# One load of x instead of two, and a shorter last load of w_down, in an attention and GLU decode kernel

## The chip, the cores and the metric

The kernel runs on one core of a Trainium2 chip. The metric is the device time of one execution in microseconds (us). All numbers of the profile come from one further execution, taken with the hardware profiler.

## The reference

Everything is float32. One token with D = 512 numbers goes through a layer norm; the result feeds an attention over a cache of 8192 keys and values for each of 32 heads of 128 numbers, and a gated linear unit (GLU) with F = 1376 hidden numbers.

```
xn = (x - mean(x)) / sqrt(var(x) + 1e-5)                 # x: 512 numbers
q  = (xn @ wq)            -> 32 heads x 128              # wq: 512 x 4096
p  = softmax(q . k_cache / sqrt(128))  over 8192 keys    # k_cache: 32 x 8192 x 128
s  = concat_heads(p @ v_cache) @ wo                      # v_cache: 32 x 8192 x 128, wo: 4096 x 512
h  = sigmoid(xn @ w_gate) * (xn @ w_up)                  # w_gate, w_up: 512 x 1376
g  = silu(h @ w_down)                                    # w_down: 1376 x 512
out = x + s * g
```

## The kernel before

**Data.** The caches are 128 MiB each, the weights some 24 MiB together. Each number is read once and used once, so nearly all that the kernel does is move them from HBM to SBUF and multiply once.

**Memory.** Three slots of 64 KB a partition (`slots[0..2]`, 8 MiB each) hold what is streamed. A load of keys takes two heads (a *pair*, 16 pairs in all, `NP`): heads 2i and 2i+1 lie on partitions 0 to 63 and 64 to 127, each partition with 128 consecutive keys. Keys of pair i go to slot i % 2, the values of each pair but the last to slot 2, in which `wq` lay at first. The values of the last pair go to slot 0, and then `w_gate`, `w_up` and the first 1280 rows of `w_down` to slot 2, and `wo`, in six pieces, to slot 1.

**Queues.** All those loads are issued by SyncE (SP), in the order of the program, each behind a wait for its slot: `load_keys(i)` waits until the scores of pair i-2 have been summed, `load_values(i-1)` until TensorE has used the values of pair i-2. `load(eng, name, dst, src, *after)` (L131 is its `dma_start`) gives each load a semaphore. ScalarE (ACT) issues the small ones: the two loads of x at the start, and `place(i)`, which spreads the two heads of a finished pair over eight partitions of `o_all`.

**The start.** x is needed in two forms. `x_col` is x as columns: 128 partitions with 4 numbers each, `x_col[p, k] = x[4p + k]`; the layer norm works on it and makes `xn`, which TensorE takes as weights. `x_row` has x as rows: partitions 0, 32, 64 and 96 hold 128 numbers each, and every other partition zero; only the last addition (L418) reads it. The layer norm is a chain that goes to and fro: VectorE sums (L180), TensorE adds over the partitions by a matmul with ones (L182), VectorE subtracts the mean and squares (L184 to L190), TensorE adds again (L192), ScalarE takes the root (L194), VectorE scales (L196, L198). Then 64 matmuls with `wq` make the queries (L206), ScalarE copies them (L211), TensorE spreads each row over the partitions (L218), and ScalarE copies that to `qb` (L225), two pairs at a time; `copies[0]` is what pairs 0 and 1 wait for.

**The pairs.** For each pair VectorE multiplies the keys in place with the queries (L281) and sums over the 128 numbers of each key (L282). TensorE, VectorE and ScalarE find the maximum and the powers (L284, L246, L276, L248, L294, L296), TensorE takes the values (64 matmuls, L255), and VectorE scales the two heads (L288, L289).

**The tail.** After the last pair TensorE makes gate and up (L356), 32 numbers of the hidden row at a time on each of four partition groups; the first 1280 columns make groups of 320, and the last 96 are in columns 320 to 351 of groups 1 to 3. For that VectorE sets group 0 of those columns to zero (L348), and TensorE waits for it. After the sigmoid and the product, eleven 32x32-block transposes (L366, L367) turn the hidden row into columns, `hid`. The down product is made of ten matmuls with 128 rows of `w_down` (`wd_t`) and one with `wd_last`. `wd_last` holds the last 128 rows of `w_down`, of which the first 32 have been taken already; `hid` is zero there.

```python
    ld_d = load(SP, "wd", wd_last, w_down[F - P:, :])           # P = 128
    ...
        ins = PE.matmul(big[0][g:g + 1, :], hid[:, c, 0:1], wd_t[:, c, :] if c < FP else wd_last, ...)
```

The sums of four partition groups are folded (L371, L377), the gate is made (L390, L392), and the product with `wo` follows, each piece as it lands (L402, then L406). L416 multiplies by the gate, L418 adds `x_row`, and SP stores the result (L422).

Of the kernel before, what the change touches and what calls it, by code (L numbers as in the profile page):

```python
# [13 lines left out]
P = 128  # L14
# [4 lines left out]
def kernel(  # L19
# [15 lines left out]
    F = w_gate.shape[1]  # L35
    KT = D // P
# [3 lines left out]
    NG = 4  # L40
    GP = P // NG
# [3 lines left out]
    NQ = H * Dh // QT  # L45
# [6 lines left out]
    FP = F // P  # L52
    FL = F - FP * P
    FW = FP * GP
    FH = FW + GP
# [4 lines left out]
    PE, DVE, ACT, SP, POOL = nc.tensor, nc.vector, nc.scalar, nc.sync, nc.gpsimd  # L60
# [8 lines left out]
    def sb(name, *shape):  # L69
        return nc.alloc_sbuf_tensor(name, [P, *shape], F32)[:]  # L70

    def bank(name, rows, cols):
        return nc.alloc_psum_tensor(name, [rows, cols], F32)[:]


    x_col, xc, sq, xn = (sb(n, KT) for n in ("x_col", "xc", "sq", "xn"))
    st, eps_t = sb("st", 8), sb("eps_t", 1)
    mx, nb, rs, rl = sb("mx", 4), sb("nb", 2), sb("rs", 1), sb("rl", 1)

# [2 lines left out]
    x_row, g_row = sb("x_row", GC), sb("g_row", GC)  # L82
    ones, ident = sb("ones", P), sb("ident", P)
# [5 lines left out]
    wd_last = q_all[:, :D]  # L89
# [7 lines left out]
    hid = o1[:, :(FP + 1) * GP].rearrange("p (c i) -> p c i", i=GP)  # L97
# [3 lines left out]
    big = [bank(f"big{i}", P, QT) for i in range(2)]  # L101
# [7 lines left out]
    def semaphore(name):  # L109
        sems.append(nc.alloc_semaphore(name))  # L110
        return sems[-1]
# [11 lines left out]
    pe, dve, act, pool = (Steps(n) for n in ("s_pe", "s_dve", "s_act", "s_pool"))  # L123
    loads = {}

    def load(eng, name, dst, src, *after):
        wait(eng, *after)
        if name not in loads:
            loads[name] = [semaphore(f"s_{name}"), 0]
        loads[name][1] += 16  # L130
        eng.dma_start(dst, src).then_inc(loads[name][0], 16)  # L131
        return loads[name][0], loads[name][1]

    def wait(eng, *steps):
        for s in steps:
            if s is not None:
                eng.wait_ge(*s)
# [7 lines left out]
    xv = x.rearrange("a b d -> (a b d)")  # L145
# [9 lines left out]
    def load_keys(i, *after):  # L155
        ld_k[i] = load(SP, f"k{i % 2}", slots[i % 2], rows_of(k_cache, i), *after)
# [5 lines left out]

    load_keys(0)
    load_keys(1)
    ld_x = load(ACT, "x", x_col, xv.rearrange("(p k) -> p k", k=KT))


    c_ones = dve(DVE.memset(ones, 1.0))
    c_xrow = dve(DVE.memset(x_row, 0.0))
    ld_xr = load(ACT, "xr", x_row[0:P:GP, :], xv.rearrange("(g c) -> g c", g=NG), c_xrow)  # L170
    c_eps = dve(DVE.memset(eps_t, EPS))
    c_id = pool(POOL.memset(ident, 0.0))
    wait(POOL, c_id)
# [2 lines left out]
    c_big = [dve(DVE.memset(t, 0.0)) for t in big]  # L176


    wait(DVE, ld_x)
    t = dve(DVE.reduce_sum(st[:, 0:1], x_col, axis=AX.X))  # L180
    wait(PE, t)
    t = pe(PE.matmul(pt[:, 0:1], ones, st[:, 0:1], start=True, stop=True))  # L182
# [19 lines left out]
    for k in range(KT):  # L202
        for b in range(NQ // NG):
            for g in range(NG):
                c = (b * NG + g) * QT
                ins = PE.matmul(big[b][g * GP:g * GP + 1, :], xn[:, k:k + 1], wq_t[:, k, c:c + QT],  # L206
                                start=(k == 0), stop=(k == KT - 1))
# [6 lines left out]
    spreads, copies = {}, {}  # L214
    for t in range(NQ):
        b, g = divmod(t, NG)
# [117 lines left out]
    wd_t = t[:, 2 * KT * F:2 * KT * F + FP * D].rearrange("p (c e) -> p c e", e=D)  # L334
    ld_g = load(SP, "wg", wg_t, w_gate.rearrange("(p k) f -> p k f", k=KT), (valued, NP - 1))
    ld_u = load(SP, "wu", wu_t, w_up.rearrange("(p k) f -> p k f", k=KT))
    load(SP, "wd", wd_t, w_down[:FP * P, :].rearrange("(p r) e -> p r e", r=FP))
    ld_d = load(SP, "wd", wd_last, w_down[F - P:, :])
    wo_t = slots[(NP - 1) % 2].rearrange("p (r e) -> p r e", e=D)
    ld_o = []  # L340
    for n, (r0, r1) in enumerate(zip((0,) + W_ENDS, W_ENDS)):
# [1 line left out]
                         summed[NP - 1] if n == 0 else None))  # L343


    g0 = (P - FL) // GP
    wait(DVE, copies[NQ - 1])
    c_zero = dve(DVE.memset(big[1][:g0 * GP, FW:FH], 0.0))  # L348
    wait(PE, c_zero)
    rows = []  # L350
    for dst, src, ld in ((big[0], wg_t, ld_g), (big[1], wu_t, ld_u)):
        wait(PE, ld)
        for c0, f0, w, g1 in ((0, 0, FW, 0), (FW, F - P, GP, g0)):
            for k in range(KT):
                for g in range(g1, NG):
                    ins = PE.matmul(dst[g * GP:g * GP + 1, c0:c0 + w], xn[:, k:k + 1],  # L356
                                    src[:, k, f0 + g * w:f0 + (g + 1) * w], start=(k == 0), stop=(k == KT - 1))
        rows.append(pe(ins))
# [22 lines left out]
    wait(PE, t, ld_d)  # L381
    for c in range(FP + 1):
        g = c % NG * GP
        ins = PE.matmul(big[0][g:g + 1, :], hid[:, c, 0:1], wd_t[:, c, :] if c < FP else wd_last,
                        start=(c < NG), stop=(c + NG > FP))
    t = to_fold(pe(ins))
    wait(DVE, t)
# [4 lines left out]
    c_gate = dve(DVE.tensor_mul(g_row, g_row, big[1][:, :GC]))  # L392
# [4 lines left out]
    for ld, r1 in zip(ld_o, W_ENDS):  # L397
        wait(PE, ld)
        for r in range(r0, r1):
            if r < W_FOLD:  # L400
                g = r % NG * GP
                ins = PE.matmul(big[0][g:g + 1, :], o_all[:, r:r + 1], wo_t[:, r, :],  # L402
                                start=(r < NG), stop=(r + NG >= W_FOLD))
                continue
            for g in range(NG):
                ins = PE.matmul(acc[g * GP:g * GP + 1, :], o_all[:, r:r + 1], wo_t[:, r, g * GC:(g + 1) * GC],  # L406
                                start=(r == W_FOLD), stop=(r == WR - 1))
# [4 lines left out]
        if r1 == W_FOLD:  # L412
            parts = to_fold(pe(ins))
        r0 = r1
    wait(DVE, pe(ins), c_gate, ld_xr)
    t = dve(DVE.tensor_mul(g_row, g_row, acc))  # L416
    wait(DVE, t)
    t = dve(DVE.tensor_add(g_row, g_row, x_row))  # L418
# [39 lines left out]
```

## Time and profile before

| what | before |
|---|---|
| time, median of 3 runs | 687.56 us (687.45 to 687.59) |
| profiled execution: span from the first to the last instruction | 685.6 us |
| what the median has over that span | 1.96 us |
| VectorE busy | 574.0 us (84%) |
| TensorE busy | 222.1 us (32%) |
| mean busy share of the 16 DMA engines by the packets of queue q1 (SP) | 99.1% |
| packets of queue q10 (ACT) | 408, with 0.02 MB |
| bytes read from HBM | 293.74 MB, 428 GB/s over the span |

The page gives no time of its own for the profiled execution, only its span. The median of the runs is 1.96 us more than that span: what lies before the first and after the last instruction. A change that shortens the span by so much is taken to shorten the time by the same.

In a timeline row the columns are: start and duration in us, engine (PEld is the weight load of TensorE; SPq and ACTq are the DMA issues of SyncE and ScalarE), line, operation, what is written from what, and in brackets the idle time before it with what ended it. In a row of DMA issues the last number is the time from issue to landing.

### The profile page before, as it was taken

Reading aid. Unit: us, or ns where it says so; the run is one execution under the profiler, and the core shown is the slowest. Engines: PE = TensorE matmul, PEld = TensorE weight load, DVE = VectorE, ACT = ScalarE, POOL = GpSimd, SP = SyncE. Lnnn points to the kernel's source line nnn. Section 1 sums busy time; section 2 is a strip of 40 time slices with the busy share of each in tenths; the row PEclk is TensorE's granted clock in tenths of the full one; section 3 lists DMA queues with packets and bytes.
Section 4 is the critical chain, followed back from the end, with each engine's and each line's share of the span. In section 5 each row is a group of like instructions: output and inputs, shape, how many; then the busy total and the mean of one; then the engine's idle time right before and its main releaser. Section 6 shows DMA issues by size and latency. Waiting matters only on the chain.

```text
span 685.6 us, 3694 instructions
## 1 busy us (share of the span) xinstructions
PE 222.1 (32%) x1570; PEld 62.7 (9%) x1570; DVE 574.0 (84%) x136; ACT 40.9 (6%) x122; POOL 0.7 (0%) x6
## 2 busy tenths in 40 slices
PE   0550230605041140505042140506042140605656
PEld 0110000101010010101001010101000010101121
DVE  0159999999999999989898989989898989989220
ACT  0040100000000000000001010000001010000010
POOL 0000000000000000000000000000000000000000
PEclk9965575757566575757557575756657575756798
DMA  9999999999999999999999999999999999999996
GB/s 375 440 445 451 428 428 428 432 428 428 428 436 444 448 440 428 428 428 436 428 428 428 440 444 451 428 432 428 432 432 428 428 440 436 451 436 428 405 434 285
DMA packets 6614, 293.84 MB, mean 429 GB/s; under 512 B 1096, under 2 KB 1104, under 8 KB 1616
## 3 DMA queue, kind: packets, MB, share of 16 engines
q1 hardware_dynamic: 6200, 293.74, 99.1%
q10 hardware_dynamic: 408, 0.02, 0.0%
q8 instruction: 4, 0.07, 0.0%
q14 instruction: 2, 0.02, 0.0%
HBM read 293.74 MB, written 0.00 MB: 428 GB/s over the span
## 4 chain that ended last, share of the span: by engine, by line
DMA 37%; DVE 30%; PE 0%; SPq 0%; issue 0%
DMA slot<-in_A_k_cache_dram 31%; DVE slot L281 15%; DVE sc L282 15%; DMA slot<-in_A_wo_dram 6%; PE acc L406 0%; SPq L131 0%; PE pt L246 0%; PE acc L377 0%; DVE g_row L416 0%; DVE g_row L418 0%; DVE mx L276 0%
## 5 line engine op out<-in xcount | busy, mean ns | idle before, releaser
L281 DVE TENSOR_TENSOR slot<-slot,q_all 128x16384 f32<-128x16384 f32 x16 | 275.5, 17217 | 38.8 <-DMA slot<-in_A_k_cache_dram 38.8
L282 DVE TENSOR_REDUCE sc<-slot 128x128 f32<-128x16384 f32 x16 | 275.5, 17220 | 0.6
L255 PE MATMUL po<-slot,weights 128*8 128x512 f32 x1024 | 146.7, 737 | 232.1 <-PEq L242 231.5
L255 PEld LDWEIGHTS po<-slot,weights 128*8 128x8 f32 x1024 | 30.3, 103 | 335.3 <-issue 334.6
L246 PE MATMUL pt<-ident,mx 128*1 128x128 f32 x32 | 8.8, 374 | 148.6 <-PEq L242 148.6
L301 ACT COPY o<-po 128x512 f32<-128x512 f32 x16 | 9.4, 586 | 385.2 <-PE po L255 385.2
L260 PE MATMUL pn<-o,pick 128*2 128x128 f32 x128 | 16.5, 272 | 12.8 <-PEq L242 12.8
L180 DVE TENSOR_REDUCE st<-x_col 128x1 f32<-128x4 f32 x1 | 0.2, 157 | 20.7 <-DMA x_col<-in_A_x_dram 20.7
L246 PEld LDWEIGHTS pt<-ident,mx 128*1 128x1 f32 x32 | 1.8, 80 | 154.1 <-issue 154.1
L288 DVE RECIPROCAL rl<-pn 2x1 f32<-2x1 f32 x16 | 2.3, 146 | 14.6 <-PE pn L260 14.6
L294 ACT ACTIVATE nb<-pm 128x2 f32<-128x2 f32 x16 | 2.8, 173 | 190.4 <-PE pm L248 190.4
L416 DVE TENSOR_TENSOR g_row<-g_row,acc 128x128 f32<-128x128 f32 x1 | 0.3, 289 | 15.3 <-PE acc L406 15.3
L296 ACT ACTIVATE weights<-sc,nb 64x128 f32<-64x128 f32 x32 | 12.8, 399 | 0.9
L260 PEld LDWEIGHTS pn<-o,pick 128*2 128x2 f32 x128 | 9.9, 84 | 29.6 <-issue 27.2
L248 PE MATMUL pm<-mx,ones 1*128 1x2 f32 x32 | 8.8, 344 | 7.4 <-PEq L242 7.4
L402 PE MATMUL big<-slot,o_all 128*1 128x512 f32 x56 | 9.4, 765 | 4.8 <-DMA slot<-in_A_wo_dram 4.8
L250 PE MATMUL pn<-rs,half 128*2 128x1 f32 x32 | 3.0, 163 | 23.5 <-PEq L242 23.5
L218 PE MATMUL big<-q_all,ones 1*128 1x512 f32 x16 | 8.8, 850 | 1.6 <-ACT q_all L225 0.8
L206 PE MATMUL big<-slot,xn 128*1 128x512 f32 x64 | 9.0, 726 | 0.8 <-DVE xn L198 0.8
L248 PEld LDWEIGHTS pm<-mx,ones 1*128 1x128 f32 x32 | 7.9, 306 | 14.4 <-issue 14.4
L276 DVE TENSOR_REDUCE mx<-pt 1x2 f32<-1x128 f32 x16 | 4.5, 278 | 5.2 <-PE pt L246 5.0
L182 PE MATMUL pt<-st,ones 128*128 128x1 f32 x2 | 0.6, 362 | 23.4 <-DVE st L180 23.4
(61 smaller groups left out, 62.1 us busy)
## 6 DMA issues: line engine op xcount, KB each, us to landing
slot<-in_A_wo_dram SPq DMA_DIRECT2D x1, 3584.0 KB, 32.5
slot<-in_B_w_gate_dram SPq DMA_DIRECT2D x1, 2752.0 KB, 16.8
slot<-in_B_w_up_dram SPq DMA_DIRECT2D x1, 2752.0 KB, 22.8
slot<-in_B_w_down_dram SPq DMA_DIRECT2D x1, 2560.0 KB, 27.3
slot<-in_A_wo_dram SPq DMA_DIRECT2D x1, 2560.0 KB, 38.2
slot<-in_A_wo_dram SPq DMA_DIRECT2D x1, 1024.0 KB, 40.2
o_all<-on ACTq DMA_DIRECT2D x32, 0.5 KB
slot<-in_A_wo_dram SPq DMA_DIRECT2D x1, 512.0 KB, 40.9
```

The costliest lines, as they stand in the source:

```text
L206: ins = PE.matmul(big[b][g * GP:g * GP + 1, :], xn[:, k:k + 1], wq_t[:, k, c:c + QT], start=(k == 0), stop=(k == KT - 1))
L218: spreads[t] = pe(PE.matmul(big[t % 2], ones[g * GP:g * GP + 1, :], q_row[g * GP:g * GP + 1, b, :], start=True, stop=True))
L246: PE.matmul(pt[0:1, :], mx[:, 0:1], ident, start=True, stop=True).then_inc(turned, 1)
L248: PE.matmul(pm, ones[:1, :], mx[:1, 1:3], start=True, stop=True).then_inc(spread_m, 1)
L255: ins = PE.matmul(po[g * GP:g * GP + 2 * HT, :], weights[:, j // HT, :], v[:, j * Dh:(j + HT) * Dh], start=(j < HT * NG), stop=(j >= NB - ...
L260: ins = PE.matmul(pn[:, :Dh], pick[:, b:2 * HT:HT], o1[:, b * Dh:(b + 1) * Dh], start=(b == 0), stop=(b == HT - 1))
L276: DVE.reduce_max(mx[:1, 1:3], pt[0:1, :].rearrange("o (e p) -> o e p", e=2), axis=AX.X).then_inc(reduced, 1)
L281: wait(DVE, dve(DVE.tensor_mul(k, k, qb[:, i:i + 1, :].to_broadcast([P, NB, Dh]))))
L282: summed[i] = dve(DVE.reduce_sum(sc[i % 2], k, axis=AX.X))
L296: ACT.activation(weights[h, :, e * HT:(e + 1) * HT], sc[i % 2][h].rearrange("p (g b) -> p g b", b=HT), AF.Exp, bias=nb[h, e:e + 1], scale= ...
L301: ACT.copy(o1, po).then_inc(copied, 1)
L402: ins = PE.matmul(big[0][g:g + 1, :], o_all[:, r:r + 1], wo_t[:, r, :], start=(r < NG), stop=(r + NG >= W_FOLD))
```

## The change

**x.** The tile `x_col` and its load are gone. VectorE clears `x_row` first, then ScalarE issues the load of x as rows; `ones` is set after that instead of before. VectorE waits for that load, and turns the rows into columns with one transpose in blocks of 32x32: number 4i + k of row g goes to partition 32g + i, column block k. The result is put in `g_row`, which is not used otherwise before the tail; `x_col` is now a view of it with one number in every 32. The wait for the load ahead of the last addition is gone.

**The last rows of w_down.** 96 rows are loaded to 96 partitions instead of 128 to 128, and the last matmul of the down product takes 96 rows. The last 96 columns of gate and up are now in groups 0 to 2 instead of 1 to 3; as many matmuls as before. L348, which set a part of a bank to zero, and the two waits around it are gone.

```diff
-    x_col, xc, sq, xn = (sb(n, KT) for n in ("x_col", "xc", "sq", "xn"))
+    xc, sq, xn = (sb(n, KT) for n in ("xc", "sq", "xn"))
...
-    ld_x = load(ACT, "x", x_col, xv.rearrange("(p k) -> p k", k=KT))
-    c_ones = dve(DVE.memset(ones, 1.0))
     c_xrow = dve(DVE.memset(x_row, 0.0))
     ld_xr = load(ACT, "xr", x_row[0:P:GP, :], xv.rearrange("(g c) -> g c", g=NG), c_xrow)
+    dve(DVE.memset(ones, 1.0))
...
-    wait(DVE, ld_x)
+    wait(DVE, ld_xr)
+    x_turned = g_row.rearrange("p (k i) -> p k i", k=KT)
+    x_col = x_turned[:, :, 0]
+    wait(DVE, dve(DVE.transpose(x_turned, x_row.rearrange("p (i k) -> p k i", k=KT))))
     t = dve(DVE.reduce_sum(st[:, 0:1], x_col, axis=AX.X))
...
-    ld_d = load(SP, "wd", wd_last, w_down[F - P:, :])
+    ld_d = load(SP, "wd", wd_last[:FL, :], w_down[F - FL:, :])
...
-    g0 = (P - FL) // GP
-    wait(DVE, copies[NQ - 1])
-    c_zero = dve(DVE.memset(big[1][:g0 * GP, FW:FH], 0.0))
-    wait(PE, c_zero)
...
-        for c0, f0, w, g1 in ((0, 0, FW, 0), (FW, F - P, GP, g0)):
+        for c0, f0, w, n in ((0, 0, FW, NG), (FW, F - FL, GP, FL // GP)):
             for k in range(KT):
-                for g in range(g1, NG):
+                for g in range(n):
...
-        ins = PE.matmul(big[0][g:g + 1, :], hid[:, c, 0:1], wd_t[:, c, :] if c < FP else wd_last,
+        n = P if c < FP else FL
+        ins = PE.matmul(big[0][g:g + 1, :], hid[:n, c, 0:1], wd_t[:, c, :] if c < FP else wd_last[:n, :],
...
-    wait(DVE, pe(ins), c_gate, ld_xr)
+    wait(DVE, pe(ins), c_gate)
```

## The prediction

> **What bounds the kernel now.** I began with the engines and the DMA rows of the page, because the kernel reads every number once.
>
> ```profile
> DMA  9999999999999999999999999999999999999996
> ...
> q1 hardware_dynamic: 6200, 293.74, 99.1%
> q10 hardware_dynamic: 408, 0.02, 0.0%
> ```
>
> The packets that SP's queue issued keep the 16 DMA engines busy for 99.1% of the span, and in the slices only the last shows a gap. ACT's queue, with the loads of x among its 408 packets, rounds to 0.0%. The next question is whether anything but bytes ends last. The chain of waits, in order of time, gives its last pieces so:
>
> ```profile
> 560.91 42.81 DMA slot<-in_A_k_cache_dram
> ...
> 603.74 17.24 DVE slot L281
> ...
> 621.00 17.23 DVE sc L282
> ...
> 639.57 40.94 DMA slot<-in_A_wo_dram
> ...
> 680.54 0.62 PE acc L406 x16
> ...
> 682.61 0.29 DVE g_row L418
> ```
>
> VectorE stands in this chain, but as a link in a circle: summed keys free a slot, the next load is issued and waits in a queue that is already full. How full is shown by the rate. The windows below run from the landing of wq to that of the first keys, and from there to the start of the last scores; the last two columns are the DMA share and GB/s.
>
> ```profile
> 0.00:22.96 22.96, 0.00 (x0) 0.00 (x0) 1.28 (x5) 1.28 (x1) 0.70 (x6) 1.00 0.98 411
> 22.96:42.28 19.32, 15.58 (x80) 4.31 (x80) 2.96 (x17) 5.10 (x13) 0.00 (x0) 0.95 1.00 434
> 42.28:603.72 561.44, 164.91 (x1103) 47.00 (x1102) 530.21 (x88) 29.00 (x96) 0.00 (x0) 0.63 1.00 433
> ```
>
> One load of keys alone moves 434 GB/s, the whole middle 433, with a DMA share of 1.00. So a step counts only if it takes bytes or packets off the DMA engines, or lets SP's queue run dry. At 434 GB/s one of 16 engines moves 27.1 GB/s, and a 64 KB row takes 65,536 / 27,100 = 2.42 us on it.
>
> **The load of x.** The start and the rows of DMA issues:
>
> ```profile
> slot<-in_A_wq_dram SPq DMA_DIRECT2D x1, 22.0
> x_col<-in_A_x_dram ACTq DMA_DIRECT2D x1, 2.0 KB, 22.1
> ...
> 0.96 0.39 SPq L131 DMA_DIRECT2D slot<-in_A_wq_dram  x1
> 0.97 0.41 ACTq L131 DMA_DIRECT2D x_col<-in_A_x_dram  x1
> 1.04 0.17 DVE L168 MEMSET ones<- 128x128 f32 x1 [1.04 <-SPq L67]
> 1.19 0.17 DVE L169 MEMSET x_row<- 128x128 f32 x1
> ...
> 1.41 0.89 SPq L131 DMA_DIRECT2D slot<-in_A_k_cache_dram  x2
> 1.42 1.11 ACTq L131 DMA_DIRECT2D x_row<-in_A_x_dram  x1
> ...
> 23.14 0.16 DVE L180 TENSOR_REDUCE st<-x_col 128x1 f32<-128x4 f32 x1 [20.65 <-DMA x_col<-in_A_x_dram]
> ...
> 26.25 9.02 PE L206 MATMUL big<-slot,xn 128*1 128x512 f32 x64 [0.81 <-DVE xn L198]
> ...
> 35.34 0.33 SPq L161 DMA_DIRECT2D slot<-in_A_v_cache_dram  x1
> ...
> 37.15 1.54 ACT L225 COPY q_all<-big 64x256 f32<-64x256 f32 x4 [1.21 <-PE big L218]
> ...
> 42.28 17.23 DVE L281 TENSOR_TENSOR slot<-slot,q_all 128x16384 f32<-128x16384 f32 x1 [13.93 <-DMA slot<-in_A_k_cache_dram]
> ...
> 76.79 0.33 SPq L131 DMA_DIRECT2D slot<-in_A_k_cache_dram  x1
> ```
>
> Removed: 128 rows of 16 bytes, eight for each engine, and the DMA that carries them. The nearest price is q10's row: under 0.05% of 16 x 685.6 us, so under 5.5 us of engine time for 408 packets, 13 ns each at most on average. Eight rows and a completion on each engine are then 9 x 13 ns = 0.12 us; if all that q10 held were x_col's, 0.34 us; if packets this small slip in for nothing, 0. I take 0.1 us, near the average.
>
> [...]
>
> Moved: the load of x as rows. It still waits for the clearing of x_row, which now comes first on VectorE (1.04 + 0.17 = 1.21 us), so it is issued about 0.2 us after x_col's old place. ACT's own queue holds nothing before it, and its next computation waited for the chain anyway. SP's keys, issued at 1.41, aren't passed: x_row is ready ahead of them by 0.2 us, or level with them. The setting of ones moves behind it and has 20 us until L182.
>
> When do the four rows land? Four rows of the tail bear on that, and on the transpose:
>
> ```profile
> 638.25 11.93 SPq L131 DMA_DIRECT2D slot<-in_A_wo_dram  x6
> ...
> 654.71 1.19 ACTq L131 DMA_DIRECT2D o_all<-on  x2
> ...
> 660.99 1.27 DVE L366 STREAM_TRANSPOSE o<-q_all 128x32 f32<-128x32 f32 x10
> ...
> 670.91 5.81 PE L402 MATMUL big<-slot,o_all 128*1 128x512 f32 x28 [4.61 <-DMA slot<-in_A_wo_dram]
> ```
>
> In the trace of before nothing waits for x_row until the end, so only bounds exist. x_col landed at 0.97 + 22.1 = 23.07 us and wq at 0.96 + 22.0 = 22.96: eight small rows on each engine finished with eight large ones. Either the two queues take turns packet by packet, or x_col stood behind all of wq. The tail decides for taking turns: the heads that ACT placed at 654.71 are used by L402 at 670.91, while SP's loads, all issued by 638.25 + 11.93 = 650.18, ran on until 680.5, where the chain has the end of wo. So x as rows, one or a few packets an engine, lands after one to three 64 KB rows: I take 5 to 9 us; from above 23 us, as x_col did.
>
> Added: one transpose of 128x128 in 32x32 blocks, before L180. The row of L366 has 1.27 us for ten transposes of 128x32, 0.127 us each; one instruction of four times that size makes 0.13 us, if the cost is by instruction, to 0.5 us, if it is by size. In that order xn is ready at about 9 + 0.5 + (26.25 - 23.14 = 3.1) = 13 us at the latest, and TensorE then waits for wq at 22.96. The queries start 26.25 - 22.96 = 3.3 us earlier. That is worth nothing: the first scores at 42.28 wait for keys. L225 had made its first two of four copies by 37.15 + 0.77 = 37.92, 4.36 us ahead. If x came late, this would be the cover: 4.36 us until VectorE slips, and then the margin of SP's queue. Keys 1 and values 0 follow at 19.32 us each, to 42.28 + 38.64 = 80.92, and the next load was issued at 76.79: 4.1 us more. The first 8.5 us of lateness cost nothing.
>
> **The last rows of w_down.** The issues and the tail:
>
> ```profile
> slot<-in_B_w_up_dram SPq DMA_DIRECT2D x1, 2752.0 KB, 22.8
> slot<-in_B_w_down_dram SPq DMA_DIRECT2D x1, 2560.0 KB, 27.3
> ...
> q_all<-in_B_w_down_dram SPq DMA_DIRECT2D x1, 256.0 KB, 28.5
> ...
> 632.86 0.43 SPq L131 DMA_DIRECT2D slot<-in_B_w_up_dram  x1
> 633.33 0.43 SPq L131 DMA_DIRECT2D slot<-in_B_w_down_dram  x1
> 633.81 0.43 SPq L131 DMA_DIRECT2D q_all<-in_B_w_down_dram  x1
> ...
> 654.68 0.09 DVE L348 MEMSET big<- 32x32 f32 x1
> ...
> 666.68 0.29 DVE L392 TENSOR_TENSOR g_row<-g_row,big 128x128 f32<-128x128 f32 x1 [0.16 <-ACT g_row L390]
> ```
>
> Removed: 32 rows of 2 KB, 65,536 bytes. From the landing of w_up (632.86 + 22.8 = 655.66) to that of wd_last (633.81 + 28.5 = 662.31) the two parts of w_down, 2816 KB, took 6.65 us: 434 GB/s, so rows of 2 KB do not slow the engines. 65,536 bytes are then 0.15 us. The load shares 6 rows to an engine instead of 8 if all 16 take part. No trace here shows a load of 96 rows, so the bounds are these. On 12 engines with 8 rows each nothing is gained; on 8 engines with 12 rows each, every one has 8 KB more to move, and 0.30 us are lost. On the other side, wd_last landed 662.31 - (633.33 + 27.3 = 660.63) = 1.68 us behind the part before it, and a quarter of that is 0.42 us gained. I keep 0.15 us gained, since the nearest row, the same load with 128 rows, ran at the full rate. [...]
>
> L348 and its two waits go: 0.09 us on VectorE, and TensorE begins gate and up up to 0.7 us earlier. The matmuls keep their number, and 96 rows instead of 128 change no column count. All this is covered: the GLU ends with L392 at 666.97, and L402 begins at 670.91 when wo lands, 3.9 us later. If that cover went, the 0.7 us would be a gain. The wait for x_row at the end had been met long before, and goes for nothing.
>
> **The sum.** Against the span: 685.6 - 0.1 - 0.15 = 685.35 us. The median of the runs lies 687.56 - 685.6 = 1.96 us above that span, and nothing in the change touches what lies outside it. So I forecast 687.3 us, 0.04% faster. A measurement of this kernel can tell about 0.2%, 1.4 us, from no change: the forecast is "no change that can be seen".
>
> **Rivals.** *x lands late* (slower). If the four rows queue behind what SP issued at about the same time, they land with the first keys, at 42.28 instead of 23.07. The chain from L180 to the first copies takes 37.92 - 23.14 = 14.8 us, with the transpose 15.2, so the first scores begin at 57.5, 15.2 us late; SP's next load slips from 76.79 to 92, the queue is dry from 80.9 on, and 11.1 us are lost for good, since the DMA engines have no slack to make it up: 698.7 us. It decides from a landing after 23.07 + 8.5 - 0.5 = 31 us. For it: x_row's issue and the keys' nearly coincide. Against it: the placed heads, which overtook a queue of loads. Chance 0.05.
>
> *The 96 rows fall on few engines* (slower). All on one engine would be 88 rows more there, 180 KB at 27.1 GB/s, 6.7 us: about 694 us. It decides (1.4 us) from 19 rows more on one engine. Against it: each load with 128 rows went at the full rate, and 96 divides by 16 too. Chance 0.03.
>
> *x_col held up the start* (faster). wq took 22.0 us from issue to landing, while the same number of bytes behind it took 19.32: 2.68 us of start. If half to all of that came from the turns with x_col, 1.34 to 2.68 us go: 684.9 to 686.2 us. For it: small packets stand between all of wq's. Against it: the window to 22.96 has a DMA share of 0.98, so the engines stood still for little of it, and q10's packets account for 0.34 us at most. Chance 0.05.
>
> **How the numbers follow.** No visible change has 0.87, the rivals 0.05, 0.03 and 0.05. The low end takes both bounds of gain: 0.34 for x_col, and for wd_last 0.42 us as above: 686.8, and 0.1 for the spread of the runs makes 686.7. The high end takes no gain for x, the 0.30 us lost for w_down, and the same spread: 688.0. The rivals beyond it hold 0.13.
>
> **What would show it.** Right: q10 falls from 408 packets to 264 (128 rows and 16 completions less) and q1 by 32; L180 runs before 10 us and TensorE starts L206 at about 23.0 with the landing of wq; the first L281 still starts at 42.3 behind keys; the loads keep 433 GB/s; the GLU ends before 667 and wo still ends last, 0.1 to 0.4 us earlier. Wrong: L281 first waits for ScalarE's copies instead of keys, or a slice early in the DMA row drops below 9, or w_down's last part lands later behind the other part than 1.7 us, or the landing of wq comes more than 1 us earlier.

## The result: 0.36% slower, and the profile after

| | before | changed |
|---|---|---|
| time, median of 5 runs | 687.45 us (687.28 to 687.59) | 690.09 us (689.80 to 690.41) |
| span of the profiled execution | 685.6 us | 688.1 us (its own time 690.01) |

The ratio is 1.0036, with a 95% interval from 1.0026 to 1.0047. The forecast was 687.3 us and no visible change; the kernel lost 2.6 us.

The rows of the changed kernel that answer to those of the prediction, from its page:

```profile
DMA  9999999999999999999999999999999999999996
...
q1 hardware_dynamic: 6168, 293.67, 99.0%
...
q10 hardware_dynamic: 264, 0.02, 0.0%
```

Fewer packets and fewer bytes (293.67 MB for 293.74), as intended, and the engines are as busy as before (99.0% of the span for 99.1): they took longer over less. So the stream of loads has no new gap; the transfers themselves are slower. Its timeline shows from where on:

```profile
1.24 1.11 ACTq L131 DMA_DIRECT2D x_row<-in_A_x_dram  x1
...
10.61 0.40 DVE L181 STREAM_TRANSPOSE g_row<-x_row 128x128 f32<-128x128 f32 x1 [8.13 <-DMA x_row<-in_A_x_dram]
...
23.04 8.89 PE L208 MATMUL big<-slot,xn 128*1 128x512 f32 x64 [9.69 <-DMA slot<-in_A_wq_dram]
...
42.26 17.23 DVE L283 TENSOR_TENSOR slot<-slot,q_all 128x16384 f32<-128x16384 f32 x1 [26.00 <-DMA slot<-in_A_k_cache_dram]
...
295.17 17.23 DVE L283 TENSOR_TENSOR slot<-slot,q_all 128x16384 f32<-128x16384 f32 x1 [2.25 <-DMA slot<-in_A_k_cache_dram]
...
604.98 17.22 DVE L283 TENSOR_TENSOR slot<-slot,q_all 128x16384 f32<-128x16384 f32 x1 [2.89 <-DMA slot<-in_A_k_cache_dram]
...
670.89 0.29 DVE L391 TENSOR_TENSOR g_row<-g_row,big 128x128 f32<-128x128 f32 x1 [0.17 <-ACT g_row L389]
...
673.26 9.63 PE L401 MATMUL big<-slot,o_all 128*1 128x512 f32 x56 [2.74 <-DMA slot<-in_A_wo_dram]
...
685.16 0.29 DVE L417 TENSOR_TENSOR g_row<-g_row,x_row 128x128 f32<-128x128 f32 x1
```

and the same rows of before that are new here:

```profile
294.47 17.23 DVE L281 TENSOR_TENSOR slot<-slot,q_all 128x16384 f32<-128x16384 f32 x1 [1.83 <-DMA slot<-in_A_k_cache_dram]
...
603.74 17.23 DVE L281 TENSOR_TENSOR slot<-slot,q_all 128x16384 f32<-128x16384 f32 x1 [3.02 <-DMA slot<-in_A_k_cache_dram]
```

Line numbers have moved: up to the pairs by two (L283 is L281), in the tail by one the other way (L391 is L392). The start went as forecast: TensorE has its queries when wq lands (23.04), and the first scores still wait for keys at 42.26. Then the loss grows with the bytes: 0.70 us by the scores at 295, 1.24 us by the last scores (604.98 for 603.74). Between these two rows lie eight pairs: (603.74 - 294.47) / 8 = 38.66 us a pair before, (604.98 - 295.17) / 8 = 38.73 us after, 0.17% more. That is too little for the column of GB/s: the window from 42.28 to 603.72 us reads 433 in both traces. The rest is lost in the tail, in a shorter time. The landings of w_down, from the rows of DMA issues and from the timeline of SyncE:

```profile
slot<-in_B_w_down_dram SPq DMA_DIRECT2D x1, 2560.0 KB, 28.2
...
q_all<-in_B_w_down_dram SPq DMA_DIRECT2D x1, 192.0 KB, 30.4
```

```profile
633.95 0.43 SPq L131 DMA_DIRECT2D slot<-in_B_w_down_dram  x1
634.43 0.43 SPq L131 DMA_DIRECT2D q_all<-in_B_w_down_dram  x1
```

The first ten parts of w_down land at 633.95 + 28.2 = 662.15, 1.52 us later than before; the 96 rows land at 634.43 + 30.4 = 664.83, 2.68 us behind them, where the 128 rows took 1.68. That is 1.0 us more for a quarter less. Both parts of the change are in this number; e4, below, has the 96 rows alone.

### The profile page after: what moved, and what is told of

Its sections match the earlier page's. It is cut to its first block, busy times and chain, and to the rows that moved or that the text cites. A ratio compares the mean times of both kernels' runs of the same rounds, so it can differ in the third digit from the quotient of the medians.

```text
span 688.1 us, 3692 instructions
## 1 busy us (share of the span) xinstructions
PE 225.1 (33%) x1570; PEld 63.4 (9%) x1570; DVE 574.4 (83%) x136; ACT 40.9 (6%) x122; POOL 0.7 (0%) x6
## 3 DMA queue, kind: packets, MB, share of 16 engines
q1 hardware_dynamic: 6168, 293.67, 99.0%
HBM read 293.67 MB, written 0.00 MB: 427 GB/s over the span
## 4 chain that ended last, share of the span: by engine, by line
DMA 37%; DVE 30%; SPq 0%; issue 0%; PE 0%
DMA slot<-in_A_k_cache_dram 31%; DVE slot L283 15%; DVE sc L284 15%; DMA slot<-in_A_wo_dram 6%; SPq L131 0%; PE pt L248 0%; PE acc L405 0%; DVE g_row L415 0%; DVE g_row L417 0%; DVE mx L278 0%
## 5 line engine op out<-in xcount | busy, mean ns | idle before, releaser
L283 DVE TENSOR_TENSOR slot<-slot,q_all 128x16384 f32<-128x16384 f32 x16 | 275.5, 17218 | 52.1 <-DMA slot<-in_A_k_cache_dram 51.9
L262 PEld LDWEIGHTS pn<-o,pick 128*2 128x2 f32 x128 | 9.9, 84 | 29.6 <-issue 27.2
## 6 DMA issues: line engine op xcount, KB each, us to landing
slot<-in_B_w_down_dram SPq DMA_DIRECT2D x1, 2560.0 KB, 28.2
```

The source lines that it names most:

```text
L262: ins = PE.matmul(pn[:, :Dh], pick[:, b:2 * HT:HT], o1[:, b * Dh:(b + 1) * Dh], start=(b == 0), stop=(b == HT - 1))
L283: wait(DVE, dve(DVE.tensor_mul(k, k, qb[:, i:i + 1, :].to_broadcast([P, NB, Dh]))))
```

## The experiments

The diff holds something that neither its words nor the prediction's sum speak of. `x_col` was the first tile that the kernel allocated, and its 4 numbers took 32 bytes of each partition. Without it every later tile lies 32 bytes lower: by the program's list of allocations the slots began at byte 16,896 (33 x 512) of a partition and now begin at 16,864. Three theories were set against each other: the **address** of the slots; the **turns** of x_col's small rows with those of wq, which might have set the engines apart from each other; and the **96 rows**. Times are medians of 10 to 12 runs (of e14 there is one) beside runs of the kernel before on the same chip.

### Address, turns or rows

`e1_after_spare`: the changed kernel, with the place kept.

```diff
-    xc, sq, xn = (sb(n, KT) for n in ("xc", "sq", "xn"))
+    _, xc, sq, xn = (sb(n, KT) for n in ("spare", "xc", "sq", "xn"))
```

> The changed kernel with an unused tile of 4 numbers a partition ahead of xc, where x_col was: all else is as changed. In the changed program every tile behind x_col lies 32 bytes lower, so the slots begin at byte 16864 of a partition and not at 16896, a multiple of 512. Address theory: the 1.2 us lost between 42 and 604 us and most of what is lost after it come back; 687.2 us if the 96 rows cost nothing of their own, 688.7 if they do (their landing was 1.0 us later on top of the rest). Turn theory (x_col's small rows, taken in turns with the rows of wq, set the engines apart from each other, and without them the loads hinder each other): the place of the tiles is nothing, 690.1 us. Row theory (96 rows on 96 partitions alone): 690.1 us.

Measured: 687.96 us, before 687.48; ratio 1.0008 (0.9999 to 1.0017). Of 2.6 us, 2.1 are back, by an unused tile. The time lies between the two that were expected of the address theory (687.2 if the 96 rows cost nothing, 688.7 if they cost what their late landing showed).

`e2_before_shift32`: the kernel before, with such a tile in front.

```diff
-    x_col, xc, sq, xn = (sb(n, KT) for n in ("x_col", "xc", "sq", "xn"))
+    _, x_col, xc, sq, xn = (sb(n, KT) for n in ("spare", "x_col", "xc", "sq", "xn"))
```

> The kernel before with an unused tile of 4 numbers a partition ahead of x_col: nothing else changes, and every tile lies 32 bytes higher, the slots at byte 16928. Address theory: slower, 688.7 to 690 us, with the loss spread over all loads: the last scores start at 605 instead of 603.7. Turn theory and row theory: no change, 687.45 us, 603.7.

Measured: 689.18 us, before 687.48; 1.0025 (1.0015 to 1.0034). The same loads, the same instructions, 1.7 us slower. Its last scores, from its timeline:

```profile
604.89 17.23 DVE L281 TENSOR_TENSOR slot<-slot,q_all 128x16384 f32<-128x16384 f32 x1 [2.87 <-DMA slot<-in_A_k_cache_dram]
```

`e3_x_alone`: the part on x, with the 128 rows and L348 as before.

> Only the part on x: one load as rows and the transpose, with 128 rows of w_down as before; the slots lie at byte 16864. Address theory: 688.7 to 689.2 us, the last scores at 605, the landing of the last rows of w_down about 0.6 us behind the part before it by the rates of the loads. Turn theory: the same 688.7 to 689.2. Row theory: 687.3 us.

Measured: 689.12 us, 1.0024 (1.0015 to 1.0034), as e2. Its last 128 rows land 1.78 us behind the part before them, near the 1.68 of before and not at the 0.6 expected. The last scores stand at 604.99:

```profile
604.99 17.23 DVE L283 TENSOR_TENSOR slot<-slot,q_all 128x16384 f32<-128x16384 f32 x1 [3.08 <-DMA slot<-in_A_k_cache_dram]
```

`e4_w_alone`: the part on w_down, with both loads of x.

> Only the part on w_down: 96 rows to 96 partitions, with both loads of x as before; the slots lie at byte 16896. Address theory: 687.3 us, last scores at 603.7, if the rows cost nothing of their own. Row theory: slower by what the landing of wd_last shows in the changed kernel, 1.0 us, or more if the pieces of wo behind it suffer: 688.4 to 689 us. Turn theory: 687.3 us.

Measured: 688.03 us, 1.0006 (0.9997 to 1.0016). By its time alone this isn't clear of no change, and it lies between what the theories expected. Its last scores start at 603.97, 0.23 us later than before, and its first piece of wo lands at 638.47 + 33.0 = 671.47, 0.72 us later than before; so about 0.5 us go in between, in the tail.

The address theory stands, and the turns fall, since e1 has no small rows and most of the loss is gone. The 96 rows remain as a second, smaller cost.

`e5_x_alone_spare`: e3 with the tile of e1, that is, the part on x with the place kept.

> The part on x alone, with an unused tile of 4 numbers in x_col's place, so that all tiles lie where they lay before (slots at byte 16896), and 128 rows of w_down. Address theory: all of the loss of the part on x goes, and what is left is the gain of 128 small rows less, 0 to 0.1 us: 687.3 to 687.5 us, against 689.1 for the same part with the tiles 32 bytes lower. Turn theory (if the place of the tiles was only a part of it): 688 us or more.

Measured: 687.36 us, before 687.57; 0.9997 (0.9988 to 1.0006). Nothing that can be seen is left of the turns. This is also the version to choose, if any: no slower than the kernel before, with one load less, and no faster that can be seen.

### How far off, and which tile

`e6_before_shift64`, `e9_before_shift128` and `e7_before_shift256` put 16, 32 and 64 unused numbers in front of the kernel before.

```diff
+    sb("spare", 16)      # 32 in e9, 64 in e7
```

> The kernel before with an unused tile of 16 numbers in front: every tile 64 bytes higher, slots at byte 16960, a multiple of 64 and no more. If rows must begin at a multiple of 64 bytes: 687.5 us, and last scores at 603.7. If they must begin at a multiple of 128, 256 or 512: as with 32 bytes, 689.2 us and 604.9.

> The kernel before with an unused tile of 32 numbers in front: every tile 128 bytes higher, slots at byte 17024, a multiple of 128 and not of 256. 64 bytes cost 1.3 to 1.5 us and 256 cost nothing. If 128 is enough: 687.5 us, last scores at 603.7; if 256 is needed: 688.9 us, about 604.9.

> The kernel before with an unused tile of 64 numbers in front: every tile 256 bytes higher, slots at byte 17152, a multiple of 256 and not of 512. If a multiple of 256 or less is what counts: 687.5 us, last scores at 603.7. If 512: 689.2 us.

| slots moved by | time | before | ratio | last scores |
|---|---|---|---|---|
| 32 bytes (e2) | 689.18 us | 687.48 | 1.0025 (1.0015 to 1.0034) | 604.89 |
| 64 bytes (e6) | 688.91 us | 687.57 | 1.0019 (1.0010 to 1.0028) | 605.00 |
| 128 bytes (e9) | 688.94 us | 687.51 | 1.0021 (1.0012 to 1.0029) | 604.95 |
| 256 bytes (e7) | 687.43 us | 687.57 | 0.9998 (0.9989 to 1.0007) | 603.67 |

The move by 256 bytes is free (687.43 us for 687.57); those by 32, 64 and 128 cost nearly the same (1.70, 1.34 and 1.43 us). The eight pairs between the scores near 295 us and the last scores say it more sharply than the times. In the ten kernels whose slots lie at their old place or 256 bytes from it (before, e1, e4, e5, e7, e8, e10, e11, e12, e14) a pair takes 38.64 to 38.66 us, in the six with the slots elsewhere (the changed kernel, e2, e3, e6, e9, e13) 38.71 to 38.73.

`e10_before_rest_moved` leaves the slots and moves what lies behind them.

```diff
+    sb("spare", 4)
     x_row, g_row = sb("x_row", GC), sb("g_row", GC)
```

> The kernel before with an unused tile of 4 numbers between the slots and x_row: the slots stay at byte 16896, all that lies behind them (x_row, the queries with wd_last, scores, o_all) moves 32 bytes. If the place of the slots is what counts, since all large loads but wd_last go there: 687.5 us. If that of the tiles VectorE and TensorE work on, or of wd_last: 688 us or more, toward 689.2.

Measured: 687.56 us, before 687.51; 1.0000 (0.9991 to 1.0009). So it is not what lies behind the slots. The small tiles ahead of them moved too in e2, but SP loads nothing into those, and it is SP's loads that land later: it is the slots, to which all its loads but the last rows of w_down go.

`e12_no_product` and `e13_no_product_shift32` ask whether VectorE has a part in it.

```diff
-        wait(DVE, dve(DVE.tensor_mul(k, k, qb[:, i:i + 1, :].to_broadcast([P, NB, Dh]))))
+    sb("spare", 4)      # in front of all tiles, e13 only
```

> The kernel before without VectorE's product of keys and queries (the scores are sums of keys alone; VectorE works 17.2 us a pair instead of 34.5, and writes nothing into the slots). It is the partner of the next kernel. The DMA engines are the bound, so 687 us, at most 1 us less.

> The same without the product, and with an unused tile of 4 numbers in front, so that the slots begin at byte 16928. If the DMA engines hinder each other by themselves when rows begin between multiples of 256: slower than its partner by the 1.7 us that the shift cost with the product. If it was VectorE's writes into the slots that met the shifted rows: as its partner.

Measured, before 687.52 us: 687.59 (1.0000, 0.9991 to 1.0010) and 689.18 (1.0024, 1.0014 to 1.0034). With half of VectorE's work gone and none of its writes in the slots, the shift costs the same 1.6 us. VectorE waits for keys in each pair of both, so its starts are landings:

```profile
217.81 17.22 DVE L281 TENSOR_REDUCE sc<-slot 128x128 f32<-128x16384 f32 x1 [7.87 <-DMA slot<-in_A_k_cache_dram]
...
604.18 17.22 DVE L281 TENSOR_REDUCE sc<-slot 128x128 f32<-128x16384 f32 x1 [8.19 <-DMA slot<-in_A_k_cache_dram]
```

```profile
217.85 17.22 DVE L282 TENSOR_REDUCE sc<-slot 128x128 f32<-128x16384 f32 x1 [7.26 <-DMA slot<-in_A_k_cache_dram]
...
605.05 17.22 DVE L282 TENSOR_REDUCE sc<-slot 128x128 f32<-128x16384 f32 x1 [8.01 <-DMA slot<-in_A_k_cache_dram]
```

Ten pairs take 386.37 us and 387.20: 38.64 and 38.72 us each, 0.21% more, from transfers alone.

### The 96 rows

`e8_before_rows1536` takes away as many bytes, but in width, and keeps 128 partitions.

```diff
-    ld_d = load(SP, "wd", wd_last, w_down[F - P:, :])
+    ld_d = load(SP, "wd", wd_last[:, :D * FL // P], w_down[F - P:, :D * FL // P])
```

> The kernel before with the last load of w_down cut in width instead of in rows: 384 of 512 numbers of each of 128 rows, so as many bytes as 96 whole rows (the last 128 columns of that block are left out and stale numbers are used). The 96 rows cost about 0.55 us with the tiles in their old places. Partition theory (96 partitions are shared among the engines in another way than 128, and hinder each other and the piece of wo behind them): nothing of it here, 687.3 us. Byte theory (a shorter load leaves the engines in other steps for wo): as with 96 rows, 688.0 us.

It leaves out the last 128 columns of these rows. Measured: 687.37 us, before 687.57; 0.9997 (0.9988 to 1.0006). `e11_w_64_and_32` is e4 with the 96 rows in two loads.

```diff
+    load(SP, "wd", wd_last[:HP, :], w_down[F - FL:F - FL + HP, :])
+    ld_d = load(SP, "wd", wd_last[HP:FL, :], w_down[F - FL + HP:, :])
```

> The part on w_down alone, tiles in their old places, but the 96 rows come in two loads, 64 rows to partitions 0 to 63 and 32 rows to 64 to 95. If any share of partitions other than that of 128 makes the engines hinder each other: 688.0 us, as with one load of 96. If it is 96, with six rows an engine, that lies badly: 687.4 us.

Measured: 688.64 us (688.13 to 691.38), before 687.51; 1.0026 (1.0015 to 1.0037), above both times expected. The twelve times fall into two groups, seven from 688.13 to 688.80 and five from 690.28 to 691.38. The one traced, 690.91, is of the second group, so its trace shows a loss of 3.4 us and not the median's 1.1; why there are two groups is open. `e14_w_behind_wo` issues the 96 rows behind wo.

> The part on w_down alone, with the load of the 96 rows issued behind all of wo instead of ahead of it; the GLU now waits for it, so the time is some 10 us longer and isn't compared, only landings. If the 96 rows upset the loads that follow them: wo runs as in the kernel before, its first piece landing 8.5 to 9.1 us after the ten parts of w_down and the rate from 655 to 672 us 430 GB/s or more, against 418 with the 96 rows ahead. If wo was slow for another reason: 418 again.

It took 700.99 us, since the GLU waits for its last rows. What is compared is the window from 655 to 672 us, in which w_down ends and the first pieces of wo land; the last two columns are DMA share and GB/s. In this order: before, e8, e4, e11, e14.

```profile
655.00:672.00 17.00, 9.02 (x150) 3.43 (x146) 3.04 (x15) 2.61 (x4) 0.00 (x0) 0.90 1.01 430
```

```profile
655.00:672.00 17.00, 9.16 (x130) 2.51 (x122) 3.04 (x15) 1.97 (x4) 0.00 (x0) 0.81 1.01 432
```

```profile
655.00:672.00 17.00, 7.79 (x111) 2.22 (x113) 3.03 (x15) 2.39 (x4) 0.00 (x0) 0.90 1.01 418
```

```profile
655.00:672.00 17.00, 8.84 (x123) 2.66 (x115) 3.04 (x15) 2.61 (x4) 0.00 (x0) 0.78 1.00 374
```

```profile
655.00:672.00 17.00, 2.62 (x60) 1.10 (x56) 2.27 (x13) 1.24 (x2) 0.00 (x0) 0.71 1.00 430
```

Where a load of 128 partitions stands ahead of wo, or none, these windows move 430 to 432 GB/s. With 96 partitions ahead it is 418, and in the one execution traced with 64 and 32 only 374, at a DMA share of 1.00 to 1.01 in all. The other traces with 128 rows lie between 425 (e2, e12) and 434 (e7), so 418 is below all of them. It comes again in e1, and with the slots moved as well, in the changed kernel, the window falls to 405, for 426 in e3. In this order, e1, e3 and the changed kernel:

```profile
655.00:672.00 17.00, 10.19 (x139) 3.09 (x135) 3.04 (x15) 2.61 (x4) 0.00 (x0) 0.80 1.01 418
```

```profile
655.00:672.00 17.00, 8.45 (x146) 3.30 (x143) 3.62 (x18) 2.61 (x4) 0.00 (x0) 0.93 1.00 426
```

```profile
655.00:672.00 17.00, 9.51 (x139) 3.14 (x128) 3.35 (x16) 2.61 (x4) 0.00 (x0) 0.90 1.01 405
```

The load of 96 rows is itself late. In e4 it lands at 634.35 + 28.8 = 663.15, 2.07 us behind the part before it (633.88 + 27.2 = 661.08), where 128 rows took 1.68 before (1.57 to 1.78 in all the traces with 128 rows):

```profile
slot<-in_B_w_down_dram SPq DMA_DIRECT2D x1, 2560.0 KB, 27.2
...
q_all<-in_B_w_down_dram SPq DMA_DIRECT2D x1, 192.0 KB, 28.8
```

```profile
633.88 0.43 SPq L131 DMA_DIRECT2D slot<-in_B_w_down_dram  x1
634.35 0.43 SPq L131 DMA_DIRECT2D q_all<-in_B_w_down_dram  x1
```

In the trace of e11 the slow transfers go on behind the load. Its first two pieces of wo land 34.5 and 41.2 us after their issue; the second was issued 0.38 us later, so the landings are 7.1 us apart.

```profile
slot<-in_A_wo_dram SPq DMA_DIRECT2D x1, 3584.0 KB, 34.5
...
slot<-in_A_wo_dram SPq DMA_DIRECT2D x1, 2560.0 KB, 41.2
```

Before, they are 32.5 and 38.2 us, with landings 6.1 us apart:

```profile
slot<-in_A_wo_dram SPq DMA_DIRECT2D x1, 3584.0 KB, 32.5
...
slot<-in_A_wo_dram SPq DMA_DIRECT2D x1, 2560.0 KB, 38.2
```

In e4 they are 33.0 and 38.7, 6.1 us apart again: there the loss is over by the landing of the first piece.

```profile
slot<-in_A_wo_dram SPq DMA_DIRECT2D x1, 3584.0 KB, 33.0
...
slot<-in_A_wo_dram SPq DMA_DIRECT2D x1, 2560.0 KB, 38.7
```

So fewer bytes are not the cause, since e8 has as few. Nor is it the rest of the part on w_down, such as the missing L348 and its waits: e14 has all of that, and with the 96 rows behind wo its wo runs at the old rate (430 GB/s, one execution). What is left is a load of 96 rows on 96 partitions that stands ahead of wo; whether the number of rows counts or the partitions they lie on was not separated. Why wo, with 128 partitions of its own, is slow behind such a load is not settled. Loads of 96 rows to other partitions weren't tried.

## Why the prediction was wrong

**The bound was right.** The DMA engines, busy for 99.0% of the span still, set the time, and VectorE, TensorE and the start had the cover that the prediction gave them: TensorE starts on wq at 23.04 for "about 23.0", the first scores at 42.26 for 42.3, and no early slice of the DMA row is below 9.

**Removing x_col: the step that failed.** The sum priced the load, its rows and its wait, and gave 0.1 us of gain. Nothing contradicts that term: with the place kept, e5 has 687.36 us for 687.57, no change that can be seen. But the edit has a fourth part, the tile, and that wasn't costed at all: 32 bytes less in front of the slots are 1.64 us (e3, against 687.48). The same step should have asked what else in the program depends on the edited line; the order of allocation was in view. "A step counts only if it takes bytes or packets off the DMA engines, or lets SP's queue run dry" was too narrow: the rate itself, 433 GB/s, was taken as fixed. Of the signs that the prediction named, only the end of wo moved with this loss, later instead of earlier; "the loads keep 433 GB/s" reads the same with it.

A shift by 128 bytes costs 1.4 us (e9), one by 256 nothing (e7), and the pairs show 0.17 to 0.21% more time. At the prediction's 2.42 us for a row of 64 KB that is an estimate of 4 to 5 ns a row. How the chip comes to lose just that is open; that it needs VectorE's writes is excluded by e12 and e13 (687.59 and 689.18 us).

**x as rows: right, a little off.** The rows were to land at 5 to 9 us; the transpose that waits for them starts at 10.61. It took 0.40 us, within 0.13 to 0.5, so the sum over x (now L182) ran at 11.05 and not before 10. The first 8.5 us of lateness being free by the prediction's sum, nothing followed from that: the first scores start at 42.26, and 42.28 before. The rival of a late x did not come about.

**The last rows of w_down: the wrong sign.** The term was 0.15 us gained, between 0.42 gained and 0.30 lost. With the slots in place, e4 and e1 stand 0.55 and 0.48 us above the kernel before, neither clear of no change by its time alone, but with the rate of the tail down from 430 to 418 in both. On shifted slots it is more: 690.09 - 689.12 (e3) = 0.97 us, with the rate down from 426 to 405. The rival with few engines had the right place. Its mechanism, rows counted on the busiest engine in the load itself, no run shows, and in the trace of e11 the slow transfers go on behind the load (the landings of wo's first two pieces 7.1 us apart, for 6.1). That the load could slow those behind it was in no term. One of the signs that the prediction had named did show: the last part lands 2.68 us behind the other, not within 1.7 (2.07 in e4). The nearest row, 128 rows at the full rate, was near in bytes and not in what mattered. That all 16 engines take part, on which the prediction's 6 rows to an engine rest, isn't contradicted: q1 lost 32 packets (6200 to 6168), as many as there are rows less, and so no completions, where q10 lost 144 (408 to 264) with x_col's load, its 128 rows and 16 completions. Which engine moves which of the 96 rows no run here shows, so the cause is open.

**L348 and the GLU.** Covered, as forecast, but the cover shrank: the GLU ended at 670.89 + 0.29 = 671.18 instead of before 667, and wo's product began 2.1 us behind it, where it was 3.9. The down product waited for the last rows and began 2.5 us later than before; its matmuls then took 4.4 us from the first to the last, for 2.7 before, and why is open. Its first rows, before and after:

```profile
662.46 2.31 PE L384 MATMUL big<-slot,o 128*1 128x512 f32 x18 [2.68 <-DVE o L367]
```

```profile
664.98 4.01 PE L383 MATMUL big<-slot,o 128*1 128x512 f32 x18 [5.31 <-DMA q_all<-in_B_w_down_dram]
```

**The sum again.** 1.64 (x, by the tiles) and 0.55 (96 rows) make 2.2 of 2.6 us. The rest, 0.4 us, is what the 96 rows cost more on shifted slots, as the 405 GB/s of the changed kernel's tail shows too; why the two add up to more than their sum is open.

## What to carry to other kernels

When a kernel is bound by its transfers, look at the addresses that its large loads go to. Here the kernel took the same time with the slots at byte 17,152 as at 16,896, both multiples of 256, and 1.3 to 1.7 us more with them at 16,864, 16,928, 16,960 and 17,024, which are none. Keep such addresses where they were measured to be free: allocate the large tiles first, or keep a spare where a small tile is removed. An edit that deletes a tile moves all that were allocated behind it, and an A/B test of that edit measures both; the control is the same edit with the place kept. A load that saves bytes by leaving out partitions has to be measured with the loads that follow it; here 96 partitions for 128 were to gain 0.15 us, and e4 stands 0.55 us above the kernel before.

## What the runs showed of the hardware

- Steady loads were slower where the rows of 64 KB began 32, 64 or 128 bytes off byte 16,896 of a partition (a multiple of 256): a pair (16.8 MB) took 38.71 to 38.73 us for 38.64 to 38.66, and the kernel 1.3 to 1.7 us more in 294 MB, while the DMA engines showed as busy as before (99.0% of the span for 99.1). 256 bytes off cost nothing (e7, 687.43 us for 687.57).
- A load of 192 KB to 96 partitions, with a quarter fewer bytes than to 128, landed later (2.07 us behind the part before it in e4, for 1.68 before), and the rate of the window around it was 418 GB/s for 430, with the slots moved 405 for 426. Two loads to 64 and 32 partitions cost 1.1 us in the median and 3.4 us, at 374 GB/s, in the execution traced. Cut in width, on 128 partitions, the same bytes cost nothing (e8, 687.37 us for 687.57).
